# Starting a second feed-forward layer five slots earlier and its last product two slots later, in a fused attention and two-layer kernel

## The chip, the cores and the metric

The kernel runs on one core of one Trainium2 chip. The metric is the device time of one execution in microseconds (us). The engines are PE (matrix products; PEld is its weight load), DVE (vector work), ACT (activations and copies), POOL and SP; in this kernel SP issues most of the DMAs and POOL issues the others.

## The reference

Attention with a local window and 32 global keys per head feeds a feed-forward layer with the activation `h * sigmoid(h)`, and that feeds a second one with `h * cos(h)`. Both layers have 2304 rows, a width of 512 and an inner width of 2048.

```python
def _moe_ref(x, w_in, w_out):
    h = x @ w_in
    g = h * (1.0 / (1.0 + np.exp(-h)))
    return (g @ w_out).astype(np.float32)

def _moe2_ref(x, w_in, w_out):
    h = x @ w_in
    g = h * np.cos(h)
    return (g @ w_out).astype(np.float32)

x = attention(...)          # (4 * 544, 512)
x = _moe_ref(x, moe_w_in, moe_w_out)
return _moe2_ref(x, moe2_w_in, moe2_w_out)
...
```

## The kernel before, in words

Each fp32 operand is split into a high and a low part, and each product is made of three matmuls: low by high, high by high, high by low. Tokens lie on the moving side. The program is written out as a plan of **slots**: `at(rank, slot, function, ...)` puts a piece of work in a slot, and the pieces are issued slot by slot, by rank within one. From slot 36 on every engine runs its instructions exactly in that order. An instruction that waits therefore holds up all that stand behind it on its engine, and that is true of SP's and POOL's DMA issues too.

**First layer.** Tokens are taken in six tiles of 512, 256, 256, 256, 384 and 512. For each of 16 blocks `f` of the inner width, `gemm1(t, f)` makes h (12 matmuls), `silu` and `split_g` make g (ACT tanh, DVE, ACT cast, DVE), and `gemm2(t, f)` adds g times the second weights into the output banks (12 matmuls), one slot pair later. A wide tile has two slots for each f, a 256 tile one. Attention units for later tiles are slipped in between. Slots 80 to 111 hold the 384 tile, slots 112 to 143 the last one. Slot 144 is called `base`.

**Weight conversion.** The second layer's weights arrive as 64-bit words. In the slots between, 64 pieces are loaded (`load_w2_words`, an SP DMA into `raw`, a ring of two buffers), prepared by ACT (`rebias`, L131 and L132), put together by DVE (`to_f32`, L138 and L142) and stored by SP (`store_w2`).

**Second layer.** Three token tiles of 768, 768 and 640 columns; the inner width is taken in 8 pairs of blocks, so there are 24 pairs `q`. The first product of a pair is a 2 by 2 block scheme with seven products of half the size (`product(q, j)`, 6 matmuls of 384 or 320 columns, one per slot), whose left operands are precomputed into DRAM (`w1c`) and brought in by POOL (`stream`). `take` moves each result from PSUM into h. From h a chain of DVE and ACT instructions makes the two rows of g: `turns`, `rest`, `cosine`, `times_h`, `split_g2` (L701 to L730). `gemm2_second(q, row, c)` multiplies g, 128 tokens by 512 (3 matmuls), spread over seven slots among the products of the next pairs. With pair q's products in slots s to s+6, the chain starts in slot s+6 and `gemm2_second` in slot s+10. Loads of output weights (`load_w2`) and of the next tile's tokens (`load_right`) are on SP. `finish(5)` stores the last output of the first layer.

Of the kernel before, what the change touches and what calls it, by code (L numbers as in the profile page):

```python
# [11 lines left out]
F32 = mybir.dt.float32  # L12
F32R = mybir.dt.float32r
I32 = mybir.dt.int32
# [9 lines left out]
NF = DFF // 128  # L24
# [24 lines left out]
def attention_then_two_ffn(  # L49
# [9 lines left out]
    nc = tc.nc  # L59
# [3 lines left out]
    work = ctx.enter_context(tc.tile_pool(name="work", bufs=1))  # L63
# [5 lines left out]
    ps_a = ctx.enter_context(tc.tile_pool(name="ps_a", bufs=4, space=PSUM))  # L69
# [42 lines left out]
    HALF = NF // 2  # L112
# [3 lines left out]
    def slot(part, f, dtype=F32):  # L116
        return wts.tile([128, 1024], dtype, tag=f"w{part}_{f}", name="w")
# [57 lines left out]
    def bank_h(name, which=None):  # L175
        if which is None:
            which = turn[0] = 1 - turn[0]
        return ps_h.tile([128, 512], F32, tag=f"h{which}", name=name)
# [368 lines left out]
    L = {}  # L547

    def open_second():
        pool = ctx.enter_context(tc.tile_pool(name="second", bufs=1))  # L550
        area = pool.tile([128, 6400], F32, name="area")
        more = pool.tile([128, 1024], F32R, name="more")
        L["t"] = [area[:, i * 768 : i * 768 + 768] for i in range(3)]
        L["c8"] = [area[:, 2304 + i * 1024 : 3328 + i * 1024] for i in range(2)]
        L["out"] = [area[:, 4352 + i * 1024 : 5376 + i * 1024].bitcast(F32R) for i in range(2)]
        L["h"] = [area[:, 2304 + i * 768 : 3072 + i * 768] for i in range(4)]
        L["k"] = [area[:, 5376:6144].bitcast(I32)]
        L["raw"] = [xp.tile([128, NP * 384], F32, tag=f"x{x}1", name="raw") for x in "hl"]
        L["x"] = {}
        L["a"] = [more[:, i * 512 : i * 512 + 512] for i in range(2)]  # L560

    def open_products():
        for f in (14, 15):
            a = slot(0, f, F32R)
            L["a"] += [a[:, 0:512], a[:, 512:1024]]

    def open_rest():
        L["k"].append(work.tile([128, 768], I32, tag="act2", name="k"))
        L["r"] = [work.tile([128, 768], F32, tag=f"act{i}", name="r") for i in range(2)]
        L["g"] = [  # L570
            (x[:, 0:768], x[:, 768:1536])
            for x in (xp.tile([128, 1536], F32R, tag=f"x{x}0", name="g") for x in "hl")
        ]

    def load_left(i):
        if i == MOVE:
# [32 lines left out]
                out=w1c[i][LEFT.index(name)], in_=o[:, c].rearrange("p s x -> p (s x)").bitcast(F32)  # L609
            )  # L610

    def stream(q):
        nc.gpsimd.dma_start(out=L["a"][q % 6], in_=w1c[q // 7 % HALF][q % 7])  # L613

    def halves_of(t):
        n = size[1][t] // 2
# [42 lines left out]
    def product(q, j):  # L659
        n = size[1][q // HALF] // 2  # L660
        whole = j in (0, 1, 3, 4, 5)
        if whole:
            CH[q, j] = bank_h("ps_p", (q + j) % 2)[:, 0:n]
        bank = CH[q, {2: 0, 6: 4}.get(j, j)]
        a = L["a"][(7 * q + j) % 6].rearrange("p (s k x) -> p s k x", s=2, k=2)
        for k in range(2):
            hi, lo = a[:, 0, k], a[:, 1, k]
            xh, xl = right_parts(q // HALF, j, k)
            nc.tensor.matmul(bank, lo, xh, start=whole and k == 0, stop=False, skip_group_check=True)  # L669
            nc.tensor.matmul(bank, hi, xh, start=False, stop=False, skip_group_check=True)  # L670
            nc.tensor.matmul(bank, hi, xl, start=False, stop=k == 1, skip_group_check=True)  # L671
# [47 lines left out]

    def g_parts(q, row):  # L720
        n = size[1][q // HALF]
        return [x[:, 0:n] for x in L["g"][1 - row]]

    def split_g2(q, row, part):
        hi, lo = g_parts(q, row)
# [30 lines left out]
    EARLY = 2 * NP  # L756
    PAUSE = 6
    LEAD, SLACK, LOADS, AHEAD, FIRST, CUT = 9, 3, 6, 8, -4, 36
    POOLED = (0, 1, 2, 3, 4, 6, 8, 10)
    head, pre, gemm, pe, post = -20, 0, 10, 20, 40  # L760
    seq = [(t, f) for t in range(len(size[0])) for f in range(NF)]
# [3 lines left out]
    base = tick[-1]  # L765
# [7 lines left out]
    def at(rank, i, fn, *args):  # L773
        plan.setdefault(i, []).append((rank, fn, args))
# [83 lines left out]

    ends = [second[seq.index((t, NF - 1))] for t in range(len(SPANS))]
    free = [s for s in range(ends[0] + 3, last + 2) if all(not e <= s <= e + 2 for e in ends)]  # L860
    order = [(f, part) for i in range(HALF) for f in (i, i + HALF) for part in range(2)]
    order += [(f, part) for i in range(HALF) for f in (i + HALF, i) for part in (2, 3)]
    for i, (f, part) in enumerate(order):
        s = free[i * len(free) // len(order)]
        at(pre + 1, s - 1, load_w2_words, f, part)
        at(post - 1, s, rebias, 1, f, part)
        at(pre, s + 1, to_f32, 1, f, part)
        at(post - 1, s + 1, store_w2, f, part)
# [9 lines left out]
    for i, (t, f) in enumerate(seq):  # L878
# [11 lines left out]
        if f == NF - 1:  # L890
            at(post, second[i] if late < 0 else base + 3, finish, t)

    tiles, pairs = len(size[1]), HALF * len(size[1])
    at(pre, base + 2, load_sine)
    at(gemm - 1, base - 6, open_products)
    at(pre - 3, base + 5, open_rest)
    for i in range(HALF):
        s, wait, step = (last + 2 + 9 * i // 2, 2, 2) if i < 6 else (base + 12 + 8 * (i - 6), 3, 3)
        at(post, s, load_left, i)
# [2 lines left out]
            at(pre + 3, s + wait + g // 2 * step, split_left, i, g)  # L902
            at(pre - 1, s + wait + 1 + g // 2 * step, store_left, i, g)
    for t in range(tiles):
        s = base + 7 * HALF * (t - 1)
        for side in range(2):
            at(post, last + 2 if t == 0 else s + 8, load_right, t, side)
        for i in range(4):
            at(pre + 4, last + 4 + i if t == 0 else s + 22 + 7 * i, right_sum, t, i)
        for j in range(7):  # L910
            s_j = last + 4 * j + 5 if t == 0 else s + 7 * HALF - 6 + j
            for k in range(2):
                at(pre - 2 if t else pre + 5, s_j, split_right, t, j, k)
    for q in range(pairs):
        s = base + 7 * q
        final = q == pairs - 1
        for j in range(7):
            at(post, s + j - 6, stream, 7 * q + j)
            at(gemm, s + j, product, q, j)
            at(post, s + j, take, q, j)  # L920
        for row, b in ((1, s + 6), (0, s + 7)):
            at(pre, b, turns, q, row)
            at(pre, b, rest, q, row, 0)
            at(pre - 1, b + 1, rest, q, row, 1)
            at(pre + (0.2 if row else 0.1), b + 1, cosine, q, row, 0)
            at(pre - 0.5, b + 2, cosine, q, row, 1)
            at(pre, b + 3, times_h, q, row)
            at(pre, b + 3, split_g2, q, row, 0)
            at(pre - 1.5, b + 4, split_g2, q, row, 1)
        blocks = size[1][q // HALF] // 128  # L930
        todo = [(row, c) for row in (1, 0) for c in range(blocks)]
        for m, (row, c) in enumerate(todo):
            s_m = s + 10 + m * 7 // len(todo)
            if q == pairs - 2:
                s_m = s + 14 + m // 5
            at(gemm + 20, s_m, gemm2_second, q, row, c)
            if q % HALF == HALF - 1 and row == 0:
                at(post + 1, s_m, finish_second, q // HALF, c)
# [109 lines left out]
```

## Time and profile before

| | |
|---|---|
| median of 3 runs | 919.82 us (918.25 to 922.47) |
| profiled execution, device time | 922.28 us |
| its span, first to last instruction | 920.5 us |
| PE busy | 875.6 us (95%) |
| DVE, ACT, POOL busy | 664.1, 520.7, 166.0 us |
| mean granted TensorE clock | 0.991 |

PE is busy for nearly the whole span, so what can be won without fewer matmuls is the time in which it stands still or runs at the lower clock. The profiled execution took 2.5 us more than the median. A busy matmul is counted with its tail: a 512-column one is shown as 0.39 us, but in an unbroken run the next starts 0.22 to 0.23 us after it.

### The profile page before, as it was taken

The numbers are of one execution on the slowest core, as the hardware profiler recorded it, in microseconds if no ns is written. First come the engines' busy times: TensorE is split into PE (matmuls) and PEld (weight loads), VectorE is DVE, ScalarE is ACT, GpSimd is POOL, SyncE is SP. The second block draws the span as 40 slices with busy tenths as digits, with TensorE's granted clock in tenths as the row PEclk, the third lists the DMA queues.
The fourth block names the chain that finished last, engine by engine and source line by source line (L and its number), as shares of the span: only waits on it lengthen the run. The fifth ranks groups of instructions, "written<-read, shape, count | busy, mean of one in ns | idle before, by whom it ended". The sixth has DMA issues, their size and how long they took to land.

```text
span 920.5 us, 16535 instructions
## 1 busy us (share of the span) xinstructions
PE 875.6 (95%) x5838; PEld 761.0 (83%) x5838; DVE 664.1 (72%) x1547; ACT 520.7 (57%) x1171; POOL 166.0 (18%) x283
## 2 busy tenths in 40 slices
PE   8899899999999999998999989999899999899997
PEld 5667678989898999987878868889789988788886
DVE  4799996688887775676477648887776767766665
ACT  4989843567575564555345445564654545544553
POOL 2220110021222120011000021222122222222220
PEclk9999999999999999999999999999999999999999
DMA  8968410566565564544665677965366444365551
GB/s 259 332 208 295 158 44 12 179 187 196 158 211 165 159 200 133 153 140 150 217 211 194 213 232 235 268 196 138 92 169 186 116 122 118 96 192 142 143 126 57
DMA packets 101985, 156.53 MB, mean 170 GB/s; under 512 B 26384, under 2 KB 40208, under 8 KB 101904
## 3 DMA queue, kind: packets, MB, share of 16 engines
q1 hardware_dynamic: 77712, 111.44, 37.1%
q0 software_dynamic: 24192, 44.05, 18.7%
q8 instruction: 46, 0.75, 0.3%
q14 instruction: 35, 0.29, 0.1%
HBM read 123.47 MB, written 31.98 MB: 169 GB/s over the span
## 4 chain that ended last, share of the span: by engine, by line
PE 64%; DVE 12%; ACT 8%; DMA 8%; issue 2%; SPq 1%; POOL 0%; ACTq 0%; DVEq 0%
PE ps_y L740 6%; PE ps_y L741 5%; PE ps_y L742 5%; PE ps_y L520 5%; DMA raw<-in_w_dram 5%; PE ps_y L521 5%; PE ps_y L522 5%; PE ps_p L669 5%; PE ps_p L670 5%; PE ps_p L671 4%; PE ps_hid L483 4%; PE ps_hid L481 4%; PE ps_hid L482 4%; DVE r L705 2%; PE ps_o L354 1%
## 5 line engine op out<-in xcount | busy, mean ns | idle before, releaser
L520 PE MATMUL ps_y<-act,w 128*128 128x256 f32 (+2 forms) x384 | 133.3, 347 | 2.4 <-ACT act L499 2.4
L522 PE MATMUL ps_y<-act,w 128*128 128x256 f32 (+2 forms) x384 | 128.1, 334 | 0.5 <-DVE act L501 0.3
L521 PE MATMUL ps_y<-act,w 128*128 128x256 f32 (+2 forms) x384 | 127.7, 332 | 0.0
L481 PE MATMUL ps_hid<-xh,w 128*128 128x256 f32 (+2 forms) x384 | 126.2, 329 | 0.0
L483 PE MATMUL ps_hid<-xl,w 128*128 128x256 f32 (+2 forms) x384 | 126.1, 328 | 0.0
L482 PE MATMUL ps_hid<-xh,w 128*128 128x256 f32 (+2 forms) x384 | 126.0, 328 | 0.0
L740 PE MATMUL ps_y<-w,g 128*128 128x512 f32 x272 | 108.8, 400 | 13.0 <-DVE g L730 12.9
L741 PE MATMUL ps_y<-w,g 128*128 128x512 f32 x272 | 108.1, 397 | 0.0
L742 PE MATMUL ps_y<-w,g 128*128 128x512 f32 x272 | 108.0, 397 | 0.0
L613 POOL DMA_DIRECT2D w<-w1c x112 | 59.4, 530 | 246.2 <-PE ps_p L671 175.2
L520 PEld LDWEIGHTS ps_y<-act,w 128*128 128x128 f32 x384 | 73.4, 191 | 14.1 <-issue 4.5
L522 PEld LDWEIGHTS ps_y<-act,w 128*128 128x128 f32 x384 | 73.7, 192 | 7.9 <-DVE act L501 2.7
L493 DVE SCALAR_TENSOR_TENSOR act<-act,ps_hid 128x256 f32<-128x256 f32 (+2 forms) x96 | 50.6, 527 | 38.6 <-ACT act L492 38.0
L481 PEld LDWEIGHTS ps_hid<-xh,w 128*128 128x128 f32 x384 | 73.5, 191 | 5.7 <-issue 0.4
L483 PEld LDWEIGHTS ps_hid<-xl,w 128*128 128x128 f32 x384 | 73.2, 191 | 5.4 <-DVE xl L367 0.3
L521 PEld LDWEIGHTS ps_y<-act,w 128*128 128x128 f32 x384 | 73.7, 192 | 4.8
L482 PEld LDWEIGHTS ps_hid<-xh,w 128*128 128x128 f32 x384 | 73.3, 191 | 5.0
L499 ACT CAST act<-act 128x256 fp32r<-128x256 f32 (+2 forms) x96 | 47.4, 494 | 51.8 <-DVE act L493 39.0
L669 PE MATMUL ps_p<-w 128*128 128x384 f32 (+1 forms) x224 | 73.7, 329 | 2.5 <-DVE area L690 0.9
L492 ACT ACTIVATE act<-ps_hid 128x256 f32<-128x256 f32 (+2 forms) x96 | 44.7, 466 | 54.4 <-PE ps_hid L483 54.1
L670 PE MATMUL ps_p<-w 128*128 128x384 f32 (+1 forms) x224 | 73.5, 328 | 0.0
L671 PE MATMUL ps_p<-w 128*128 128x384 f32 (+1 forms) x224 | 73.2, 327 | 0.0
(139 smaller groups left out, 1957.2 us busy)
## 6 DMA issues: line engine op xcount, KB each, us to landing
w<-w1c POOLq DMA_DIRECT2D x112, 256.0 KB, 2.9
w<-in_w_dram SPq DMA_DIRECT2D x32, 512.0 KB, 7.3
raw<-in_w_dram SPq DMA_DIRECT2D x64, 256.0 KB, 3.2
more<-w1c POOLq DMA_DIRECT2D x56, 256.0 KB, 2.9
w2f<-w SPq DMA_DIRECT2D x64, 128.0 KB, 3.1
qk<-in_units_dram SPq DMA_DIRECT2D x24, 320.0 KB, 3.9
w1c<-area SPq DMA_DIRECT2D x28, 256.0 KB, 2.4
w1c<-w SPq DMA_DIRECT2D x28, 256.0 KB, 2.6
```

The lines of the kernel that those rows point to most:

```text
L481: nc.tensor.matmul(h, lo[:, ws], xh[:, k, :], start=k == 0, stop=False)
L482: nc.tensor.matmul(h, hi[:, ws], xh[:, k, :], start=False, stop=False)
L483: nc.tensor.matmul(h, hi[:, ws], xl[:, k, :], start=False, stop=k == NP - 1)
L520: nc.tensor.matmul(o, lo[:, ds_], gh, start=f == 0 and d % per == 0, stop=False, skip_group_check=True)
L521: nc.tensor.matmul(o, hi[:, ds_], gh, start=False, stop=False, skip_group_check=True)
L522: nc.tensor.matmul(o, hi[:, ds_], gl, start=False, stop=f == NF - 1, skip_group_check=True)
L669: nc.tensor.matmul(bank, lo, xh, start=whole and k == 0, stop=False, skip_group_check=True)
L670: nc.tensor.matmul(bank, hi, xh, start=False, stop=False, skip_group_check=True)
L671: nc.tensor.matmul(bank, hi, xl, start=False, stop=k == 1, skip_group_check=True)
L740: nc.tensor.matmul(y, gl, hi, start=begin_, stop=False)
L741: nc.tensor.matmul(y, gh, hi, start=False, stop=False)
L742: nc.tensor.matmul(y, gh, lo, start=False, stop=end)
```

## The change

1. All of the second layer but the loads and the precomputation of its left operands and weights starts five slots earlier: `onset = base - 5` takes the place of `base`. The first five products of pair 0 stand among the last four `gemm1` and `gemm2` of the first layer. Pair 0 uses two banks of another pool (`L["bank"]`) than the first layer's h.
2. `LAG = 12`: `gemm2_second` of a pair begins in slot s+12, not s+10. A third buffer for g is opened. The intermediate tiles `k` and `r` move to other places.
3. The streamed left operand has no ring of six buffers any more. It goes into the unused last 256 columns of the two tiles that hold the right operand of product j, as two DMAs of half the size.
4. The 64 weight conversions are spaced otherwise: one in each free slot up to the start of the 384 tile, then two in three slots. The plan has 28 of them in slots 80 to 111 before and 20 now; six come from slot 112 on, where none stood before. The load of a piece may be issued two slots ahead and not one.

Except for the streams, which are twice as many, each engine has the same instructions as before, in another order.

```diff
-        area = pool.tile([128, 6400], F32, name="area")
-        more = pool.tile([128, 1024], F32R, name="more")
+        area = pool.tile([128, 6912], F32, name="area")
...
-        L["k"] = [area[:, 5376:6144].bitcast(I32)]
+        L["k"] = [area[:, 5376 + i * 768 : 6144 + i * 768].bitcast(I32) for i in range(2)]
...
+        L["bank"] = [ps_a.tile([128, 512], F32, tag="a", name="ps_p") for _ in range(2)]
...
+    def open_third():
+        L["g"].append([work.tile([128, 768], F32R, tag=f"act{i}", name="g") for i in (1, 2)])
...
-    def stream(q):
-        nc.gpsimd.dma_start(out=L["a"][q % 6], in_=w1c[q // 7 % HALF][q % 7])
+    def left_parts(j):
+        return [L["x"][j, k][:, 768:1024] for k in range(2)]
+
+    def stream(q, j):
+        for i, part in enumerate(left_parts(j)):
+            nc.gpsimd.dma_start(out=part, in_=w1c[q % HALF][j][:, i * 256 : i * 256 + 256])
...
-            CH[q, j] = bank_h("ps_p", (q + j) % 2)[:, 0:n]
+            CH[q, j] = (bank_h("ps_p", (q + j) % 2) if q else L["bank"][j % 2])[:, 0:n]
...
-        return [x[:, 0:n] for x in L["g"][1 - row]]
+        return [x[:, 0:n] for x in L["g"][(2 * q + 1 - row) % 3]]
...
+    LAG = 12
...
+    slow = [s for s in range(ends[3] + 3, base) if (s - ends[3]) % 3 != 2 and not ends[4] <= s <= ends[4] + 2]
+    times = [s for s in free if s < ends[3]] + slow
...
-        s = free[i * len(free) // len(order)]
-        at(pre + 1, s - 1, load_w2_words, f, part)
+        s = times[i]
+        ready = max([times[i - 2] + 1 if i > 1 else 0, s - 2] + [e + 1 for e in ends if e < s])
+        at(pre + 1, ready, load_w2_words, f, part)
...
+    onset = base - 5
...
-        s = base + 7 * q
+        s = onset + 7 * q
...
-            at(post, s + j - 6, stream, 7 * q + j)
+            at(post, s + j - 6 if q else max(s + j - 6, last + 4 * j + 6), stream, q, j)
...
-            s_m = s + 10 + m * 7 // len(todo)
+            s_m = s + LAG + m * 7 // len(todo)
```

**PE, the first `gemm2_second` of pair 0.** Before, these rows stand there; `w_6351` and `w_6354` hold the right operand of product 3 of pair 1, `w_6549` the streamed left one.

```order
L669 MATMUL ps_p_6801<-w_6351,w_6549 128x384
L670 MATMUL ps_p_6801<-w_6351,w_6549 128x384
L671 MATMUL ps_p_6801<-w_6351,w_6549 128x384
L669 MATMUL ps_p_6801<-w_6354,w_6549 128x384
L670 MATMUL ps_p_6801<-w_6354,w_6549 128x384
L671 MATMUL ps_p_6801<-w_6354,w_6549 128x384
L740 MATMUL ps_y_6808<-w_6452,g_6732 128x512
```

Now it follows on product 5 of pair 1, whose right operand is in `w_6529` and `w_6532`, with the left one in the same two tiles.

```order
L671 MATMUL ps_p_6828<-w_6529,w_6532 128x384
L672 MATMUL ps_p_6828<-w_6529 128x384
L673 MATMUL ps_p_6828<-w_6529 128x384
L671 MATMUL ps_p_6828<-w_6532 128x384
L672 MATMUL ps_p_6828<-w_6532,w_6529 128x384
L673 MATMUL ps_p_6828<-w_6532,w_6529 128x384
L742 MATMUL ps_y_6835<-w_6453,g_6715 128x512
```

The consumer of g has moved two products further from the product that its chain starts from.

**SP, the end of the first layer.** `x_5` is the last output of the first layer, `raw<-x` the tokens of the second tile (`load_right`), `w2f_1_111` and `w2f_1_95` the output weights of blocks 9 and 1 (`load_w2`). Lines with - are of before, with + of the change.

```order
 L534 DMA x_5_91<-y 128x512 x4
+L634 DMA raw<-x_2_88 128x4x256
+L634 DMA raw<-x_3_89 128x4x128 x2
+L634 DMA raw<-x_4_90 128x4x256
 L152 DMA w<-w2f_1_111 128x512
-L632 DMA raw<-x_2_88 128x4x256
-L632 DMA raw<-x_3_89 128x4x128 x2
-L632 DMA raw<-x_4_90 128x4x256
 L152 DMA w<-w2f_1_95 128x512
```

The weights of block 9 were issued ahead of the four token loads, and now stand behind them.

**POOL, the streams in the middle of the second layer**, with the names that each issue waits for. Before:

```order
L613 DMA w<-w1c_6_130 128x512 [waits DMASW0_49,PE_49]
L613 DMA w<-w1c_0_131 128x512 [waits DMASW1_49,PE_49]
L613 DMA w<-w1c_1_132 128x512 [waits DMASW2_49,PE_49]
L613 DMA w<-w1c_2_133 128x512 [waits DMASW3_49,PE_49]
L613 DMA more<-w1c_3_134 128x512 [waits DMASW4_49,PE_49]
```

Now:

```order
L615 DMA w<-w1c_4_128 128x256 [waits DMASW0_49,PE_49]
L615 DMA w<-w1c_4_128 128x256 [waits DMASW1_49]
L615 DMA w<-w1c_5_129 128x256 [waits DMASW2_49,PE_49]
L615 DMA w<-w1c_5_129 128x256 [waits DMASW3_49]
L615 DMA w<-w1c_6_130 128x256 [waits DMASW4_49,PE_49]
L615 DMA w<-w1c_6_130 128x256 [waits DMASW5_49]
```

The names DMASW0 to DMASW7 go round, so that an issue waits for the DMA eight issues back: eight streams back before, four streams back now.

## Rows read from the trace of the kernel before

**Rows 1.** Stages: busy us of each engine, granted clock, DMA share, GB/s.

```profile
354.70:441.90 87.20, 80.10 (x569) 74.74 (x568) 56.47 (x164) 45.40 (x130) 8.54 (x8) 1.00 0.48 148
441.90:531.40 89.50, 86.37 (x373) 70.41 (x371) 57.59 (x107) 40.84 (x78) 3.40 (x6) 0.98 0.61 210
531.40:920.50 389.10, 369.46 (x1848) 325.89 (x1848) 270.26 (x389) 204.12 (x304) 85.86 (x162) 0.99 0.56 154
```

**Rows 2.** PE's waits in 531.4 to 920.5: us, times, longest.

```profile
PE ps_y L740 <- DVE g L730: 12.9, 10, 3.5
PE ps_p L669 <- DVE act L493: 1.5, 1, 1.5
PE ps_p L669 <- DVE area L690: 0.9, 1, 0.9
PE ps_p L669 <- ACT area L678: 0.8, 1, 0.8
```

**Rows 3.** PE's waits in 354.7 to 441.9, the 384 tile.

```profile
PE ps_o L347 <- POOL pgt L210: 6.2, 4, 2.3
```

**Rows 4.** ACT by line in the 384 tile: busy us, mean ns, idle before.

```profile
L131 ACT ACTIVATE raw<-raw 128x256 f32<-128x256 f32 x26 | 11.4, 439 | 29.9 <-DMA raw<-in_w_dram 27.5 <-DVE st L268 1.3 <-DVE w L142 1.1
```

**Rows 5.** Timeline of SP and ACT, one round of a conversion buffer.

```profile
436.15 0.33 SPq L126 DMA_DIRECT2D raw<-in_w_dram  x1
...
439.21 0.43 ACT L131 ACTIVATE raw<-raw 128x256 f32<-128x256 f32 x1 [1.57 <-DMA raw<-in_w_dram]
...
441.53 0.33 SPq L126 DMA_DIRECT2D raw<-in_w_dram  x1
```

**Rows 6.** Windows of 2 us, columns as in group 1.

```profile
652.00:654.00 2.00, 0.00 (x0) 0.00 (x0) 0.73 (x2) 2.00 (x5) 0.53 (x1) 1.00 0.58 160
654.00:656.00 2.00, 0.78 (x2) 0.69 (x3) 2.00 (x4) 0.16 (x1) 0.00 (x0) 0.71 0.22 69
656.00:658.00 2.00, 2.00 (x7) 1.52 (x6) 1.10 (x2) 1.28 (x3) 0.00 (x0) 0.50 0.00 0
658.00:660.00 2.00, 2.00 (x11) 1.86 (x10) 2.00 (x4) 1.41 (x3) 0.40 (x1) 0.94 0.00 0
...
788.00:790.00 2.00, 2.00 (x8) 2.00 (x7) 1.43 (x3) 1.52 (x5) 0.00 (x0) 0.50 0.00 0
```

**Rows 7.** Timeline of PE: start us, us, instruction, idle before it.

```profile
648.74 0.33 PE L669 MATMUL ps_p<-w 128*128 128x384 f32 x1
648.91 0.34 PE L670 MATMUL ps_p<-w 128*128 128x384 f32 x1
...
649.79 0.39 PE L740 MATMUL ps_y<-w,g 128*128 128x512 f32 x1
650.01 0.40 PE L741 MATMUL ps_y<-w,g 128*128 128x512 f32 x1
...
909.30 0.50 PE L740 MATMUL ps_y<-w,g 128*128 128x512 f32 x1 [0.32 <-DVE g L730]
```

**Rows 8.** Timeline of ACT and DVE: first and last piece of pair 0's chain.

```profile
544.64 0.85 ACT L701 ACTIVATE area<-area 128x768 int32<-128x768 f32 x1 [3.24 <-DVE area L688]
...
552.47 0.96 DVE L730 TENSOR_TENSOR g<-r,g 128x768 fp32r<-128x768 f32 x1 [1.27 <-ACT g L728]
```

**Rows 9.** Timeline of DVE at the start of the last tile.

```profile
460.24 0.96 DVE L640 TENSOR_TENSOR area<-raw 128x768 f32<-128x768 f32 x1 [4.17 <-DMA raw<-x]
```

**Rows 10.** PE's waits in 441.9 to 531.4, the last tile.

```profile
PE ps_y L520 <- ACT act L499: 1.6, 1, 1.6
```

**Rows 11.** DMA issues of 545 to 560: count, KB each, median us to landing.

```profile
w<-w2f SPq DMA_DIRECT2D x4, 256.0 KB, 10.0
w<-w1c POOLq DMA_DIRECT2D x4, 256.0 KB, 6.0
```

**Rows 12.** DMA queue of POOL, and its issues, in 531.4 to 920.5.

```profile
q0 software_dynamic: 23616, 43.00, 43.1%
...
w<-w1c POOLq DMA_DIRECT2D x108, 256.0 KB, 2.9
```

More of the change, by code (lines that the diff above doesn't have):

```diff
@@ L556, in open_second @@
         L["h"] = [area[:, 2304 + i * 768 : 3072 + i * 768] for i in range(4)]
-        L["k"] = [area[:, 5376:6144].bitcast(I32)]
+        L["k"] = [area[:, 5376 + i * 768 : 6144 + i * 768].bitcast(I32) for i in range(2)]
         L["raw"] = [xp.tile([128, NP * 384], F32, tag=f"x{x}1", name="raw") for x in "hl"]
         L["x"] = {}
-        L["a"] = [more[:, i * 512 : i * 512 + 512] for i in range(2)]
     def open_products():
-        for f in (14, 15):
-            a = slot(0, f, F32R)
-            L["a"] += [a[:, 0:512], a[:, 512:1024]]
+        L["bank"] = [ps_a.tile([128, 512], F32, tag="a", name="ps_p") for _ in range(2)]
     def open_rest():
-        L["k"].append(work.tile([128, 768], I32, tag="act2", name="k"))
-        L["r"] = [work.tile([128, 768], F32, tag=f"act{i}", name="r") for i in range(2)]
+        L["r"] = [slot(0, NF - 2)[:, 0:768], work.tile([128, 768], F32, tag="act0", name="r")]
         L["g"] = [
@@ L662, in product @@
         if whole:
-            CH[q, j] = bank_h("ps_p", (q + j) % 2)[:, 0:n]
+            CH[q, j] = (bank_h("ps_p", (q + j) % 2) if q else L["bank"][j % 2])[:, 0:n]
         bank = CH[q, {2: 0, 6: 4}.get(j, j)]
-        a = L["a"][(7 * q + j) % 6].rearrange("p (s k x) -> p s k x", s=2, k=2)
+        a = [x.rearrange("p (k x) -> p k x", k=2) for x in left_parts(j)]
         for k in range(2):
-            hi, lo = a[:, 0, k], a[:, 1, k]
+            hi, lo = (x[:, k] for x in a)
             xh, xl = right_parts(q // HALF, j, k)
@@ L891, in attention_then_two_ffn @@
             at(post, second[i] if late < 0 else base + 3, finish, t)
+    onset = base - 5
     tiles, pairs = len(size[1]), HALF * len(size[1])
     at(pre, base + 2, load_sine)
-    at(gemm - 1, base - 6, open_products)
-    at(pre - 3, base + 5, open_rest)
+    at(gemm - 1, onset, open_products)
+    at(pre - 3, base + 1, open_rest)
+    at(pre - 3, base + 5, open_third)
     for i in range(HALF):
@@ L904, in attention_then_two_ffn @@
     for t in range(tiles):
-        s = base + 7 * HALF * (t - 1)
+        s = onset + 7 * HALF * (t - 1)
         for side in range(2):
```

## The prediction

> **What bounds the kernel now.** I read the windows by stage first. PE is busy for 80.1 of 87.2 us in the 384 tile, 86.4 of 89.5 in the last tile of the first layer and 369.5 of 389.1 in the second layer [rows 1]. The reader is to see that PE is the bound everywhere, that no matmul is taken away, and that 7.1, 3.1 and 19.6 us of standing still are all there is to win in these stages, with the low clock besides.
>
> The view of waits, engine PE, then tells what PE stands for. In the second layer it is g: ten waits, 12.9 us, the longest 3.5, and three shorter ones ahead of products at the seam of the two layers [rows 2]. In the 384 tile it is four waits for POOL's part of the attention keys [rows 3]. POOL there waits for ACT; so I looked at ACT by line: it stands 27.5 us for the landing of raw weight words [rows 4]. The last view is that of 2 us windows, for the clock: after PE had done nothing in 652 to 654, the granted clock is 0.71, 0.50 and 0.94 in the three windows from 654 on, which is 1.2 GHz for part of each; at 788 it is 0.50 again [rows 6].
>
> **How long a slot is.** Matmuls of 384 columns start 0.17 us apart, those of 512 columns 0.22 [rows 7] (0.23 over longer runs). A product is 6 x 0.17 = 1.04 us, a block of `gemm2_second` 3 x 0.23 = 0.69. A pair of a 768 tile has 7 products and 12 blocks: 7.3 + 8.3 = 15.6 us, 2.23 for a slot.
>
> A stall costs more than its shown gap: a 512-column matmul is drawn 0.39 long but followed after 0.22 [rows 7], so some 0.17 us of pipelining is lost with each wait. I add that per wait removed.
>
> **The change, part by part.**
>
> *Distance 12.* The chain from the first `turns` to the last `split_g2` of a row lasts from 544.64 to 552.47 + 0.96, which is 8.8 us [rows 8]. Before, between the product that it starts from (j = 5) and the first `gemm2_second` PE has products 6, 0, 1, 2, 3 and 6 blocks of the pair before: 5.2 + 4.1 = 9.3 us. That is just above 8.8, so any other work on DVE or ACT makes PE wait. The longest wait of 3.5 us means a chain of about 12.8. Now seven products and 12 blocks lie between: 15.6 us. Even the longest chain fits, with 2.8 us to spare. Only the last pair keeps its wait of 0.3 [rows 7], since behind its products nothing is left to fill with. So 12.9 - 0.3 = 12.6 us go, and 9 x 0.17 = 1.5: **-14.1**. The bounds: all of it, or -8 if the longest waits (where the next tile's operands are split by the same engines) stay in part. The third g buffer makes this distance possible and costs no instruction. What is late next is nothing on PE: h has four buffers, and is read before it is written again.
>
> *Clock.* Each of the two low stretches, at 654 and 788, loses (0.29 + 0.50 + 0.06) x 2 = 1.7 us of full clock [rows 6], of which some falls in the wait itself; I take 1.5 each, **-3.0**. The waits before them should be gone. From below it is nothing, if the clock falls after some other wait, from above -3.4.
>
> *Seam.* The first product waited 1.5 us for the first layer's last bank of h, two others 0.9 and 0.8 for the `take` two products back [rows 2]. Pair 0 now has its own banks, and its first five products stand between `gemm1` and `gemm2` pieces, where a `take` has over 2 us. But products 2 to 4 of pair 1 now stand in slots with nothing beside them, and `take(1, 1)` is behind `finish(5)`'s copy on DVE. I leave 1.5 us of waits: 3.2 - 1.5, and two lost restarts of 0.17: **-2.0**, between -3.7 and 0. Pair 0's chain has 7 products and four half `gemm2` of 1.4 us before its consumer, 12.8 us against 8.8 and the load of the sine table.
>
> *384 tile.* A buffer of the conversion ring makes a round in 441.53 - 436.15 = 5.4 us: 3.1 from the issue to ACT's start, ACT, DVE, next issue [rows 5]. With two buffers that is 2.7 us for each conversion, and 28 of them make 75 of the stage's 87.2 us, while ACT has little else. Since ACT takes its work in order, the attention keys stand behind such a wait. With 20 conversions the ring needs 54 us, and each load is out two slots ahead (over 4 us against 3.1). The 6.2 us of waits [rows 3] should nearly go: 6.2 - 0.5, and 4 x 0.17: **-6.4**, between -6.9 and -2 (part of the lateness is of the attention itself).
>
> *Last tile of the first layer.* Six conversions come into it, each two instructions of 0.44 us or a little less on ACT [rows 4] and as many on DVE, whose share there is 57.6 of 89.5 us [rows 1]. But five of them fall where DVE has just stood 4.17 us for the first token load and PE 1.6 in turn [rows 9, 10]. That wait stays. Five more conversions are 4.3 us of DVE in seven slots of some 2.7 us, in which by its mean share it has 12 of 19 us to do; part falls into its waits for ACT's cast. A g of this tile has a slot pair (5.4 us) of room, so I take **+0.5**, between 0 and +4.
>
> *Weights behind tokens.* SP issues the output weights of block 9 behind four token loads. Loads of such weights in that crowd took 10.0 us [rows 11]. ACT and DVE split them three slots later, 6.7 us; ACT then stands 3.3 us in its queue, and behind it the cosines of pair 1 and a `take`, behind DVE's half `take(2, 1)`. PE wants that bank two slots on, about 3.4 us after it could be read; 3.3 + 0.6 + 0.7 + 0.5 for wait, cast, difference and take leave 1.7. I take **+2.0**, between 0 and +5.
>
> *Streams.* 336 DMAs of 128 KB in place of 168 of 256 KB. POOL is busy for 85.9 of 389.1 us [rows 1] with 162 of these issues, and twice that fits. Its DMAs fill 43.1% of the DMA engines [rows 12]; by the bytes that stays, and even if every packet of half the size took as long as a whole one it would be 86%. The wait on a product is for the one seven back, not six, so a stream has a slot more. An issue now waits for the DMA four streams back. A stream lands after 2.9 us as a rule and after 6.0 in the crowd [rows 11, 12]; four in flight are one in 0.7 and one in 1.5 us, against a slot of 2.23. **0**, between 0 and +7.
>
> By the Trainium skill ("DMA: Bandwidth & Descriptors", section "Anatomy of one DMA — SWDGE (gpsimd) path") such a DMA has a fixed part of about 2.0 us and then its bytes at 436 GB/s: 2.6 us for 256 KB, which the trace's 2.9 agrees with, and 2.3 for a half. If the fixed parts came one behind the other, a stream would take 4.6 us, and the second layer 168 x 2.4 = 400 us more. The trace speaks against that: 162 landings of 2.9 us are 470 us, more than the 389 in which they lay, so they overlap.
>
> The sum: -14.1 - 3.0 - 2.0 - 6.4 + 0.5 + 2.0 = -23.0. From the profiled 922.3 that gives 899.3; the profiled run was 2.5 us above the median, so **897**.
>
> **The rivals.**
>
> *Given back.* The six conversions and the late weights cost their upper ends (+9 in place of +2.5): 903. For it speaks that DVE and ACT run in order and that a wait of 1.6 us already stands there [rows 10]; against it the free third of DVE in that stage. To this belongs that half of the gain in the 384 tile stays away: 900 to 906.
>
> *The g waits stay.* The chain could be late because ACT and DVE are late altogether, not because it starts late; then two more slots only move the wait. With 6 us of it left and one low clock: 905. Against it: DVE is busy 270 of 389 us and ACT 204 [rows 1], so they do not fall behind from pair to pair.
>
> *Streams bound the second layer; it ends slower.* The place is POOL's issue, which waits for the landing four streams back. The gain of 23 us spread over 168 slots is 0.14 us a slot, so it decides when a stream takes more than 2.37 us, a landing of 9.5 us throughout. At 10.0 us, which SP's loads show in the crowd [rows 11], a slot takes 2.5: 168 x 0.27 = 45 more, 942. If only some 28 slots of the crowd are so, +8: 905. Against it: 2.9 us as a rule [rows 12]. The Trainium skill ("DMA: Bandwidth & Descriptors", section "Bandwidth") asks for DMAs of 1 MiB and more, and would lead here too.
>
> *It does nothing.* If PE's waits only changed their names, 920. Against it: they are waits for work that stands a known distance ahead.
>
> **How the numbers follow.** The forecast, 890 to 901, has a chance of 0.68; given back, 900 to 906, 0.17; the g waits in part, or streams in the crowd, about 905, 0.09; streams as the bound 0.04; no change 0.02. The likeliest is 897. The lower end: all terms at their best make -28.1, 891.7 after the correction, and some 2 us are left for a run with fewer low clocks; the upper end takes in the second and part of the third case: 889 to 906 holds about 0.85. A change of 0.5%, 4.6 us, is about what a measurement of this kernel can tell from none. Faster 0.94, same 0.02, slower 0.04.
>
> **What would show it.** Waits of PE for g should be one of 0.3 us and none at the tile changes; the 2 us windows should show 1.00 in the second layer. ACT's wait for raw words in the 384 tile should fall from 27.5 us to a few, and the tile should take 80 to 81 us. After the token loads at the seam there should be an ACT wait of 3 to 4 us for weights. It would be wrong if products wait for streams, or if the start of the last tile shows new waits for g of several us.

## The result, and the profile after

The changed kernel took 910.64 us (median of 4 runs, 907.50 to 912.56) beside 921.03 us (4 runs, 918.25 to 922.47) for the kernel before: a ratio of 0.9887, 95% interval 0.9847 to 0.9928. It is faster by 10.4 us, a little over 1%. The forecast was 897, between 889 and 906: the sign was right, the size was not, and the time lies outside the range.

The profiled execution took 909.52 us with a span of 907.5, so 13.0 us of span are gone where the sum had 23.0. (It was 1.1 us below its median, the one before 2.5 above the median of the three runs I had; these 3.6 us and the missing 10.0 make the 13.6 between 897 and 910.6.)

First the stages of the changed kernel, in the columns of [rows 1]: the 384 tile, the last tile with the products that now stand in it, and the rest of the second layer.

```profile
358.10:436.20 78.10, 78.10 (x568) 75.08 (x567) 52.42 (x151) 41.57 (x118) 8.37 (x8) 1.00 0.44 135
436.20:516.80 80.60, 76.38 (x333) 61.23 (x332) 54.26 (x104) 39.26 (x79) 6.57 (x12) 1.00 0.72 237
516.80:907.50 390.70, 375.80 (x1891) 330.49 (x1889) 276.95 (x402) 206.48 (x312) 170.99 (x324) 1.00 0.62 157
```

The 384 tile has no idle PE left: 78.10 of 78.10 us. In the second layer the clock is 1.00 throughout, but PE still stands for 14.9 us, 4.1 of them after its last matmul (4.1 before, too). The waits of PE there, the answer to [rows 2] (L742 is what L740 was, L671 the first matmul of a product, L682 to L688 are lines of `take`):

```profile
PE ps_p L671 <- DVE area L686: 5.6, 5, 2.3
PE ps_p L671 <- DVE area L682: 1.7, 3, 0.8
PE ps_p L671 <- DVE area L688: 1.4, 2, 1.1
PE ps_p L671 <- ACT area L684: 1.2, 2, 0.8
PE ps_y L742 <- DVE g L732: 0.6, 1, 0.6
```

The ten waits for g are down to one of 0.6, where one of 0.3 was forecast. In their place stand twelve waits, 9.9 us, of a kind that [rows 2] has twice: a product waits until DVE or ACT has taken the result two products back out of the same PSUM bank. The last tile of the first layer has four waits for ACT's cast of g where [rows 10] had one:

```profile
PE ps_y L520 <- ACT act L499: 4.2, 4, 1.4
```

To see where the time went I cut the span at the start of the first matmul of a stage, the same matmul in each kernel, read from PE's timeline. Before the seam's second cut the changed kernel has issued three blocks of `gemm2_second` fewer; these 2.1 us come back at the end, so they are moved there in the table. The first of the ten waits for g lies ahead of pair 2, so 1.9 us of the -14.1 (the wait and its tail of 0.17) belong to the seam:

```profile
553.49 0.50 PE L740 MATMUL ps_y<-w,g 128*128 128x512 f32 x1 [1.77 <-DVE g L730]
```

| stage, us | before | after | forecast | measured |
|---|---|---|---|---|
| up to the 384 tile | 354.68 | 358.13 | 0 | +3.45 |
| 384 tile | 87.17 | 78.12 | -6.4 | -9.05 |
| last tile, its first 13 blocks | 74.35 | 76.69 | +0.5 | +2.34 |
| seam, from there to the first product of pair 2 | 45.40 | 39.25 (+2.1) | -1.9 (-2.0 + 2.0 - 1.9) | -4.05 |
| pairs 2 to 23 and the end | 358.90 | 355.30 (-2.1) | -15.2 | -5.7 |

Most of what is missing is in the last line. Windows of pairs 2, 3 and 4 show where, first of before, then of after with pair 5 behind them (columns as in [rows 1]):

```profile
561.60:578.40 16.80, 15.97 (x80) 14.06 (x78) 14.77 (x25) 10.44 (x16) 3.72 (x8) 1.00 0.71 207
578.40:595.10 16.70, 15.99 (x80) 13.92 (x78) 13.64 (x23) 9.88 (x16) 3.72 (x8) 1.00 0.86 254
595.10:612.50 17.40, 16.03 (x80) 14.09 (x80) 13.90 (x20) 9.36 (x13) 3.72 (x8) 1.00 0.80 243
```

```profile
552.20:568.30 16.10, 15.96 (x79) 14.04 (x78) 10.62 (x15) 9.29 (x14) 7.38 (x15) 1.00 0.87 244
568.30:587.40 19.10, 17.11 (x80) 13.70 (x79) 15.49 (x25) 9.50 (x14) 7.42 (x15) 1.00 0.82 241
587.40:606.70 19.30, 16.19 (x80) 13.91 (x79) 15.82 (x26) 10.44 (x17) 7.35 (x15) 1.00 0.82 231
606.70:622.40 15.70, 15.70 (x80) 14.11 (x79) 12.62 (x17) 9.02 (x13) 7.40 (x15) 1.00 0.77 194
```

An unbroken pair takes 15.7 us, as in the last row. Pairs 3 and 4 take 19.1 and 19.3, together 4.3 us more than before. DVE's work (third busy figure) was even over the three pairs, 14.8, 13.6 and 13.9; now it is 10.6, 15.5 and 15.8, as much as an unbroken pair is long. The timeline of DVE just before one of the waits, and PE's wait:

```profile
589.59 1.55 DVE L590 TENSOR_TENSOR w<-w 128x256 f32<-128x256 f32 x4
591.05 1.02 DVE L599 TENSOR_TENSOR w<-w 128x512 fp32r<-128x512 f32 x2
591.99 0.95 DVE L707 SCALAR_TENSOR_TENSOR r<-area,r 128x768 f32<-128x768 int32 x1
592.86 0.69 DVE L165 TENSOR_TENSOR w<-w 128x512 fp32r<-128x512 f32 x1
593.46 0.95 DVE L642 TENSOR_TENSOR area<-raw,area 128x768 f32<-128x768 f32 x1
594.33 0.55 DVE L682 TENSOR_TENSOR area<-area,ps_p 128x384 f32<-128x384 f32 x1
```

```profile
594.93 0.45 PE L671 MATMUL ps_p<-w 128*128 128x384 f32 x1 [0.78 <-DVE area L682]
```

Without a gap in 4.7 us DVE sums left operands (L590) and splits them (L599), does a part of the chain (L707), splits output weights (L165) and sums the next tile's tokens (L642); the take (L682) is last. The first, second and fourth of these are side work whose slots count from `base`. By `onset = base - 5` the pairs moved five slots against it, and the left operands of the last two pairs now fall into the pairs that also have the next tile's sums.

### The profile page after: what moved, and what is told of

Same layout as the page of the kernel before. It is cut to its first block, busy times and chain, and to the rows that moved or that the text cites. A ratio compares the mean times of both kernels' runs of the same rounds, so it can differ in the third digit from the quotient of the medians.

```text
span 907.5 us, 16685 instructions
## 1 busy us (share of the span) xinstructions
PE 872.6 (96%) x5838; PEld 757.5 (83%) x5838; DVE 665.4 (73%) x1547; ACT 517.9 (57%) x1171; POOL 254.1 (28%) x451
## 4 chain that ended last, share of the span: by engine, by line
PE 72%; DVE 11%; DMA 5%; ACT 4%; issue 2%; SPq 1%; POOL 0%; DVEq 0%; ACTq 0%
PE ps_y L520 6%; PE ps_y L522 6%; PE ps_y L521 5%; PE ps_y L743 5%; PE ps_y L744 5%; PE ps_y L742 5%; PE ps_hid L481 5%; PE ps_hid L483 5%; PE ps_hid L482 5%; PE ps_p L671 5%; PE ps_p L672 5%; PE ps_p L673 5%; PE ps_o L354 2%; DMA w<-w2f 2%; PE ps_s L252 1%
## 5 line engine op out<-in xcount | busy, mean ns | idle before, releaser
L615 POOL DMA_DIRECT2D w<-w1c x336 | 177.6, 534 | 272.3 <-PE ps_p L673 194.2
L671 PE MATMUL ps_p<-w 128*128 128x384 f32 (+1 forms) x336 | 111.4, 331 | 10.3 <-DVE area L686 5.6
L672 PE MATMUL ps_p<-w 128*128 128x384 f32 (+1 forms) x336 | 110.2, 328 | 0.0
L673 PE MATMUL ps_p<-w 128*128 128x384 f32 (+1 forms) x336 | 109.8, 327 | 0.0
L743 PE MATMUL ps_y<-w,g 128*128 128x512 f32 x272 | 107.5, 395 | 0.0
L744 PE MATMUL ps_y<-w,g 128*128 128x512 f32 x272 | 107.2, 394 | 0.0
L742 PE MATMUL ps_y<-w,g 128*128 128x512 f32 x272 | 106.3, 391 | 0.6 <-DVE g L732 0.6
L703 ACT ACTIVATE area<-area 128x768 int32<-128x768 f32 (+1 forms) x48 | 38.9, 811 | 103.9 <-DVE area L690 67.5
L493 DVE SCALAR_TENSOR_TENSOR act<-act,ps_hid 128x256 f32<-128x256 f32 (+2 forms) x96 | 50.6, 527 | 53.2 <-ACT act L492 52.7
L520 PEld LDWEIGHTS ps_y<-act,w 128*128 128x128 f32 x384 | 73.2, 191 | 16.5 <-ACT act L499 5.9
L209 POOL TENSOR_SCALAR pgt<-tg 32x512 fp32r<-32x512 f32 (+1 forms) x32 | 22.0, 688 | 225.0 <-DVE tg L203 155.0
L671 PEld LDWEIGHTS ps_p<-w 128*128 128x128 f32 x336 | 63.1, 188 | 24.2 <-DVE area L686 7.7
L522 PEld LDWEIGHTS ps_y<-act,w 128*128 128x128 f32 x384 | 73.2, 191 | 7.9 <-DVE act L501 2.8
```

What stands on the lines that cost most here:

```text
L520: nc.tensor.matmul(o, lo[:, ds_], gh, start=f == 0 and d % per == 0, stop=False, skip_group_check=True)
L522: nc.tensor.matmul(o, hi[:, ds_], gl, start=False, stop=f == NF - 1, skip_group_check=True)
L615: nc.gpsimd.dma_start(out=part, in_=w1c[q % HALF][j][:, i * 256 : i * 256 + 256])
L743: nc.tensor.matmul(y, gh, hi, start=False, stop=False)
L744: nc.tensor.matmul(y, gh, lo, start=False, stop=end)
```

## The experiments

All times are medians, beside the kernel before on the same chip; its medians in the three batches are 920.95, 922.27 and 921.52. The changed kernel's 910.64 is of a batch of its own (921.03 before), so differences to it go across batches. The durations of stages are of the one profiled execution of each.

**The distance of the second product** (distance 10). The changed kernel with one number put back.

```diff
-    LAG = 12
+    LAG = 10
```

> The changed kernel with LAG = 10, the distance of before; the rest of the change stays. If the longer distance only changed the name of a part of the waits (theory 'moved'): waits for g of about 8 to 10 us come back, those for takes fall from 10 to about 5, the second layer is 3 to 5 us longer, about 914. If the distance is worth what was forecast (14 us, with 3 for the clock): about 924. If it is worth nothing: 910.6.

923.34 us, ratio 1.0015 (0.9985 to 1.0046): the whole gain is gone. PE's waits for g are back:

```profile
PE ps_y L742 <- DVE g L732: 16.2, 11, 3.6
```

So the distance is worth 12.7 us in the medians. In the profiled executions it is 9.6, and 12.2 when counted from the seam on (406.8 beside 394.6; stretches of low clock at 579 and 651 are part of it). It does what was forecast of it, but is worth less than the 14.1 + 3.0. Beside the waits for g, those for takes are 2.2 us here and not 9.9: a part of the waits only changed its name.

**The spacing of the conversions alone** (spacing). The kernel before with part 4 of the change and nothing else.

> The kernel before with nothing but the new spacing of the 64 weight pieces. The 384 tile should take 78 us and not 87. Theory 'the last tile gives part back': the last tile is 2 to 4 us longer than the 74.4 of before with waits of PE for ACT's cast, the whole about 914 to 916. Rival 'the seam takes it all': what is gained in the 384 tile comes back as waits at the seam and in the second layer, about 919 to 921.

916.66 us, ratio 0.9945 (0.9917 to 0.9973), about 4.3 us. The 384 tile takes 78.12 us, exactly as in the changed kernel: this term belongs to the spacing alone. The last tile already has three waits for the cast of g, 3.1 us.

**Half streams.** The kernel before, each stream as two DMAs of 128 KB into its old ring.

```diff
-        nc.gpsimd.dma_start(out=L["a"][q % 6], in_=w1c[q // 7 % HALF][q % 7])
+        for i in range(0, 512, 256):
+            nc.gpsimd.dma_start(out=L["a"][q % 6][:, i : i + 256], in_=w1c[q // 7 % HALF][q % 7][:, i : i + 256])
```

> The kernel before with one thing changed: each stream of a left operand is issued as two DMAs of 128 KB instead of one of 256 KB, into the same ring of six buffers. Theory 'streams are free': 920 to 922, no product waits for a DMA, and pairs 2 to 4 take what they took before (50.9 us). Rival 'streams cost' (more issues on POOL and more packets slow the other loads): pairs 2 to 4 grow by 1 us or more and the time by 3 or more.

922.04 us, ratio 0.9996 (0.9966 to 1.0026); pairs 2 to 4 take 16.79, 16.69 and 15.75 us, and no product waits for a DMA. The issues land after 2.4 us:

```profile
w<-w1c POOLq DMA_DIRECT2D x216, 128.0 KB, 2.4
```

Twice the number costs nothing here. By the Trainium skill ("DMA: Bandwidth & Descriptors", section "Measured (HBM→SBUF, 128 partitions, SWDGE, issued from GpSimd)") DMAs should be batched to 1 MiB or more; that is a rule for bandwidth, and these streams are needed one in a slot of 2.23 us. The landing of 2.4 us is near 2.3, an estimate from the fixed part and the bytes that the same page of the Trainium skill gives (section "Anatomy of one DMA — SWDGE (gpsimd) path").

**Takes before the side work** (takes first). The changed kernel with the side work of the second layer ranked behind the takes of its slot, in the same slots.

```diff
-            at(pre, s, split_w_hi, 1, f, 1)
+            at(post + 1 if i else pre, s, split_w_hi, 1, f, 1)
...
-        at(pre + 2, s + wait, left_sums, i)
+        at(pre + 2 if i < 6 else post + 2, s + wait, left_sums, i)
...
-                at(pre - 2 if t else pre + 5, s_j, split_right, t, j, k)
+                at(post + 5 if t else pre + 5, s_j, split_right, t, j, k)
```

> The changed kernel, with the second layer's side work (left_sums and split_left of pairs 6 and 7, right_sum and split_right of the later tiles, split_w of the output weights) issued behind the take of its slot and not ahead of it. Theory 'in order': PE's waits for takes (10 us in the changed kernel) arise because side work stands ahead of the take on DVE and ACT; pairs 3 and 4 then fall from 19.1 and 19.3 us to about 16.5, pairs 7 and 15 to about 16, the waits for takes in the second layer from some 9 us to under 3, and the time from 910.6 to about 904. Theory 'DVE is full': DVE has 15.5 us of work in these pairs, a pair without waits takes 15.7, so order can't help; pairs 3 and 4 stay above 18.5 and the time within 2 us of 910.6.

908.73 us, ratio 0.9852 (0.9804 to 0.9899), which can't be told from the changed kernel. Pair 4 falls from 19.32 to 17.81 us, but pair 3 is still 20.27 (a stretch of low clock lies in it) and pairs 8 to 14, the first of the next tile among them, take 2.4 more. The order within a slot is at most a part of it; the amount of work in these pairs stays as it was.

**Spread.** The changed kernel with the side work in other slots: the left operands of the last two pairs 14 slots apart, and the sums of the next tile's tokens later.

```diff
-        s, wait, step = (last + 2 + 9 * i // 2, 2, 2) if i < 6 else (base + 12 + 8 * (i - 6), 3, 3)
+        s, wait, step = (last + 2 + 9 * i // 2, 2, 2) if i < 6 else (base + 10 + 14 * (i - 6), 3, 3)
...
-            at(pre + 4, last + 4 + i if t == 0 else s + 22 + 7 * i, right_sum, t, i)
+            at(pre + 4, last + 4 + i if t == 0 else s + (26, 39, 44, 47)[i], right_sum, t, i)
```

> The changed kernel, with the side work of the second layer put elsewhere: the left operands of the last two pairs come to slots that spread them over the pairs instead of lying in pairs 3 and 4, and the right operands of the second and third tile are prepared towards the end of the tile before, not in its middle. Theory 'piled up' (by starting five slots earlier the second layer moved against this side work, which fixed slots hold; DVE now has too much in pairs 3 and 4, and the taking of products stands behind it): pairs 2 to 4 fall from the 54.5 us of the changed kernel to 48.5 to 49.5, the waits for DVE's and ACT's taking there mostly go, and the time falls to 905 to 906. Rival 'DMA crowd' (the side work waits for its loads, wherever it stands): pairs 2 to 4 stay at 53 us or more and the time within 2 us of the changed kernel's 910.6.

906.00 us, ratio 0.9824 (0.9777 to 0.9870). Windows of pairs 2, 3 and 4:

```profile
552.60:570.20 17.60, 15.97 (x79) 14.04 (x78) 12.89 (x21) 9.34 (x14) 7.39 (x15) 1.00 0.92 263
570.20:585.90 15.70, 15.70 (x79) 14.11 (x79) 12.91 (x18) 9.60 (x14) 7.40 (x15) 1.00 0.93 271
585.90:602.70 16.80, 16.00 (x79) 14.04 (x78) 13.70 (x23) 9.30 (x14) 7.41 (x15) 1.00 0.61 154
```

DVE's work is even again (12.9, 12.9, 13.7), and the three pairs take 50.1 us and not 54.5. The DMA share is higher in the first two (0.92 and 0.93), so a busier DMA does not by itself hold the pairs up.

**Not earlier.** The changed kernel with `onset = base`: no overlap, all else as changed.

> The changed kernel with onset put back to base, so that the second layer starts where it did, with the distance of 12, the streams and the conversions of the change. Theory 'piled up': the side work is back in its old place beside the pairs, so that pairs 2 to 4 fall from 54.5 us to 48 to 50, while the seam loses what overlapping had won (2 to 4 us), and the whole comes to 908 to 912. Rival 'the longer distance makes the takes late by itself': pairs 2 to 4 stay at 53 us or more and the whole comes to 913 to 917.

906.71 us, ratio 0.9838 (0.9796 to 0.9880). Pairs 2, 3 and 4:

```profile
556.00:571.70 15.70, 15.70 (x79) 14.03 (x78) 13.77 (x23) 9.99 (x16) 7.38 (x15) 1.00 0.79 220
571.70:587.80 16.10, 16.03 (x80) 13.89 (x78) 14.07 (x23) 9.97 (x16) 7.46 (x15) 1.00 0.95 277
587.80:604.00 16.20, 16.20 (x79) 14.01 (x79) 13.99 (x20) 9.42 (x14) 7.33 (x15) 1.00 0.93 255
```

PE has no wait in them, at the same distance of 12. So the distance does not make these takes late; the five slots do. At the tile changes the waits for takes stay: pairs 7 and 15 take 18.60 and 17.26 us, as in the changed kernel. The seam takes 43.86 us here against 39.25: the overlap wins 4.6 us there and spends 6.5 in pairs 2 to 4. Some 1.7 of the 4.6 are a stretch of low clock in this seam, amid its waits:

```profile
549.00:551.00 2.00, 1.32 (x4) 1.32 (x5) 1.57 (x4) 0.83 (x1) 1.08 (x3) 0.56 1.17 373
```

The time is below what I expected (908 to 912), but its interval overlaps that of the changed kernel, so whether the overlap as it stands loses something or wins nothing is not settled.

**Late pieces.** The changed kernel with the last five conversions later in the last tile.

```diff
+    slow = [s for s in slow if s <= last] + list(range(last + 14, base, 2))
     times = [s for s in free if s < ends[3]] + slow
```

> The changed kernel, with the last five weight pieces in slots 126 to 134 and not 117 to 123. Theory 'pieces': the four waits of PE for ACT's cast in the last tile (4.2 us) come from these five pieces, two ways: on ACT and DVE, and on SP ahead of the stores of the left operands; one wait of 1.5 us stays, and the last tile goes from 76.7 to about 74 us, the whole to about 907 to 908. Rival 'crowd': the waits come from the token loads and the stores alone; no change, 910 to 911.

909.07 us, ratio 0.9847 (0.9794 to 0.9900), which can't be told from the changed kernel. The last tile takes 77.6 us (a stretch of low clock lies in it) and still has 4.7 us of waits for the cast, but not the same ones. The changed kernel has four at 20, 27, 34 and 41 us from the start of the tile; here the first stays, the other three (2.9 us) are gone, and a new one stands at 74, behind a wait of ACT for the load of another left operand:

```profile
501.98 1.05 ACT L598 CAST w<-w 128x512 fp32r<-128x512 f32 x2 [5.39 <-DMA w<-w2f]
506.41 0.50 PE L520 MATMUL ps_y<-act,w 128*128 128x512 f32 x1 [2.83 <-ACT act L499]
```

ACT's waits in these 13 blocks for the stores of left operands, first of the changed kernel, then here:

```profile
ACT area L598 <- DMA w1c<-area: 11.1, 7, 4.0
ACT area L598 <- DMA w1c<-area: 4.5, 4, 1.9
```

So the place of the five conversions does matter for the three waits in the middle, as the theory "pieces" had it, and the tile wins little or nothing because another wait comes up; what makes that load late is open.

**Sums later.** The changed kernel with the first use of the second layer's first tokens two slots later (they are those of its first tile; the expectations call them the second tile's).

```diff
-            at(pre + 4, last + 4 + i if t == 0 else s + 22 + 7 * i, right_sum, t, i)
+            at(pre + 4, last + 6 + i if t == 0 else s + 22 + 7 * i, right_sum, t, i)
...
-            s_j = last + 4 * j + 5 if t == 0 else s + 7 * HALF - 6 + j
+            s_j = last + 4 * j + 5 + 2 * (j == 0) if t == 0 else s + 7 * HALF - 6 + j
```

> The changed kernel with the first work on the second tile's tokens (right_sum and the first split_right at the start of the last tile of the first layer) two slots later. Theory 'token load' (DVE stands in front of a load that has not landed, and the first layer's activation waits behind it): DVE's 3.6 us for the tokens nearly goes, the first of PE's four waits for the activation goes too, and the last tile falls from 76.7 to 74.5 to 75.5 us; the time is 908 to 909.5. Rival 'stores' (the waits come from the stores of the sums, which ACT waits for later): the tile stays within 0.5 us of 76.7.

907.05 us, ratio 0.9826 (0.9771 to 0.9880), the last tile 74.58 us with a stretch of low clock in it. In the changed kernel, DVE stands for the tokens and the activation (L493) waits behind it, then PE:

```profile
453.95 0.96 DVE L642 TENSOR_TENSOR area<-raw 128x768 f32<-128x768 f32 x1 [3.60 <-DMA raw<-x]
454.83 0.68 DVE L493 SCALAR_TENSOR_TENSOR act<-act,ps_hid 128x512 f32<-128x512 f32 x1
...
456.21 0.49 PE L520 MATMUL ps_y<-act,w 128*128 128x512 f32 x1 [1.29 <-ACT act L499]
```

Two slots later the tokens are there, and the tile has one wait (one to three in the three kernels below):

```profile
458.44 0.95 DVE L642 TENSOR_TENSOR area<-raw 128x768 f32<-128x768 f32 x1
...
468.53 0.50 PE L520 MATMUL ps_y<-act,w 128*128 128x512 f32 x1 [1.80 <-ACT act L499]
```

One profile would not settle this, for the tile varies by up to 1.7 us between kernels in which it is alike. Over all of them: without the mend (changed kernel, takes first, distance 10, spread, not earlier) it takes 75.5 to 76.9 us, mean 76.4, and with it (this kernel and the three below) 73.8 to 75.6, mean 74.8. The ranges just touch, and the means put the standing for tokens at some 1.6 us of the tile. The spacing alone had brought three waits where before had one, and late pieces took three away; both causes act on ACT's cast, and the wait that is left is not put down to either.

**Both mends, and two variants.** *Spread and sums* joins spread and sums later. *Base and sums* is not earlier with sums later. *Rights behind* is spread and sums, with `split_right` of the later tiles ranked behind the takes (the last lines of the diff of takes first).

> The changed kernel with both mends that earlier runs bear out: the side work spread over the pairs, and the first work on the second tile's tokens two slots later. If the two losses are separate ones (side work on DVE in pairs 3 and 4; DVE standing before the token load in the last tile), the gains add: the last tile 74 to 75 us, pairs 2 to 4 at 49 to 50.5, and a median of 902.5 to 905. Rival: the time lost only moves from one to the other, and the median stays at 906 to 907.

> The changed kernel with onset put back to base (no overlap of the layers) and the first work on the second tile's tokens two slots later. By the theory that the overlap wins about 4 us at the seam once its side work is out of the way, this is behind the spread version by 0 to 3 us: 903.5 to 906. Rival (overlap wins nothing even when mended): it equals or beats the spread version.

> As the kernel with the side work spread and the sums later, and besides, the preparing of the next tile's right operands (split_right) ranked behind the taking of products. If the remaining waits at the two tile changes come from the order on DVE, pairs 7 and 15 fall from 18.6 and 17.3 us to 17 and 16.3 and the median by 1 to 2.5 us; if the operands are then late for the next tile's first products, the pairs after the change grow by as much and the median stays.

| on one chip | median, us | runs | ratio to before | interval |
|---|---|---|---|---|
| spread and sums | 901.35 | 897.25 to 904.16 | 0.9779 | 0.9745 to 0.9813 |
| base and sums | 903.35 | 902.30 to 912.13 | 0.9818 | 0.9776 to 0.9859 |
| rights behind | 901.05 | 900.27 to 902.36 | 0.9778 | 0.9749 to 0.9807 |

The two mends add: they gave 4.6 and 3.6 us below the changed kernel's median apart, and 9.3 together, and the interval of the ratio doesn't touch that of the change, which those of the two alone still overlap. This version beats both kernels. Beside base and sums, the overlap with its side work spread is worth 2.0 us, but the intervals overlap. Rights behind brings pairs 7 and 15 from 18.59 and 17.25 us to 17.48 and 16.33, and pairs 8 and 16, with which the next tile starts, from 15.96 and 14.65 to 16.85 and 15.53: what is won is given back within a pair, and the median stays, as the second half of its expectation said.

## Why the prediction was wrong, step by step

**The step that failed** is in *Distance 12*: "What is late next is nothing on PE: h has four buffers, and is read before it is written again." I looked at h, the output of the takes, and not at the PSUM bank that a take sets free, although *Seam* prices two such waits. A product needs the take of two products back, one slot of PE's time after it could be read, and takes stand in DVE's queue behind side work. The five slots, too, have a term at the seam alone, and none for the side work that stays in its slots while the pairs move. So waits for takes, 9.9 us, stand where those for g, 12.9 us, had stood, and -14.1 - 3.0 came out as -7.6 (-5.7 in the pairs and -1.9 at the seam). With the 3.0 of the clock counted as won, *Distance 12* is about -4.6, beyond its bound of -8.

Two places are shown. Pairs 2 to 4 take 54.5 us, where 47.1 (three unbroken pairs) was implied, and 48.0 without the five slots and 50.1 with the work spread: this loss is that of the five slots. Pairs 7 and 15, at the tile changes, take 2.9 and 1.6 us more than unbroken ones, in waits for takes, with the five slots and without; at distance 10 PE waits for g alone in these two pairs, so the distance uncovered those waits. My bound of -8, "if the longest waits stay in part", named the place and the engines, under another wait's name.

**Behind it stands a wrong use of an average.** Against the rival that the waits stay I wrote that DVE is busy 270 of 389 us. The average is right and still holds (277 of 391); in two pairs the share is 0.8 of a stretch that its own lateness has drawn out.

**Clock.** Right in this profile: no low stretch after 517. It is not so in every execution. *Sums later* has the same second layer, and in its profile the clock falls at 602 behind the 2.3 us wait for a take in pair 4, which takes 20.9 us there and not 19.3:

```profile
602.00:604.00 2.00, 2.00 (x7) 1.61 (x6) 1.36 (x3) 0.50 (x1) 1.05 (x2) 0.51 1.03 341
```

In the first part, for which I had no term, the profile of after has three such stretches and the one of before two, of some 1.7 us each [rows 6]. PE is busy there for 342.35 us and not 339.69, with the same matmuls, which is most of the +3.45; the idle time grew by 0.8 only. Profiles of kernels with the same first part have from one to five such stretches, so a single profile can't say whether the change has a share in it.

**384 tile.** The mechanism was right, and the term of -6.4 was mis-sized: -9.05, beyond its bound of -6.9. I had counted four waits, 6.2 us; the stage had a fifth, for ACT's cast of g, which went with them:

```profile
PE ps_y L520 <- ACT act L499: 0.8, 1, 0.8
```

The five show 7.0 us, so each cost 0.4 us that isn't drawn, where I had added 0.17; a part of that is told below, the rest is open. ACT's wait for raw words fell from 27.5 us [rows 4] to 2.1 in this line of ACT:

```profile
L131 ACT ACTIVATE raw<-raw 128x256 f32<-128x256 f32 x20 | 8.8, 438 | 2.2 <-DMA raw<-in_w_dram 2.1
```

**Last tile.** +0.5 was mis-sized; it measured +2.3, and the before it is compared with had a stretch of low clock at 464 in it, some 1.6 us, so +3.9 without it (half streams, with the first layer of before and no low stretch there, has 72.29, which makes +4.4). My upper bound was +4. I had seen DVE stand for the tokens [rows 9] and counted that standing as room for the conversions; it is the start of a delay that they prolong, for moving either of the two takes waits away. And I had counted the conversions as work of ACT and DVE alone: ACT's waits for the stores of left operands, 2.4 us before, are 7.7 with the spacing alone and 11.1 with the change.

**Seam.** -2.0 was right: without the wait for g, PE's waits there fell from 3.3 us to 1.6, where 1.5 was to be left. That the stage measured -4.05 and not -1.9 is the next term. **Weights behind tokens**, +2.0: the wait on ACT is there, 2.30 us and not 3 to 4,

```profile
557.26 0.62 ACT L161 CAST w<-w 128x512 fp32r<-128x512 f32 x1 [2.30 <-DMA w<-w2f]
```

but the view shows no wait of PE from there to 576, and pair 2 takes 16.1 us, 0.4 over an unbroken one: little or nothing of the +2.0 reached PE.

**Streams**, 0: right, shown by half streams, and no product of the changed kernel waits for one. By the time, the case that came nearest is *given back*, at its upper end of 906 and beyond it, though by takes more than by the two causes that I named. By the mechanism, *it does nothing* was nearer than its chance of 0.02 says: a large part of PE's waits changed their names.

## What to carry to other kernels

When a stage is moved in a plan written by slots, look at what stays behind: work whose slots count from a fixed point comes to lie on other pairs, and the load of each in-order engine has to be added up pair by pair, not over the stage. When a long wait is taken away, list every other resource that the same instruction needs (here the PSUM bank of two products back) and the margin of each, for the old wait had hidden them. Work that waits for a load should stand where the load has landed, above all on an engine that the critical work shares.

## What the runs showed of the hardware

A wait of PE costs more than its shown gap. The rows around one, after a block of `gemm2_second`, matmuls and then the weight loads:

```profile
575.48 0.39 PE L744 MATMUL ps_y<-w,g 128*128 128x512 f32 x1
576.56 0.45 PE L671 MATMUL ps_p<-w 128*128 128x384 f32 x1 [0.69 <-DVE area L682]
576.84 0.34 PE L672 MATMUL ps_p<-w 128*128 128x384 f32 x1
577.02 0.35 PE L673 MATMUL ps_p<-w 128*128 128x384 f32 x1
```

```profile
575.25 0.19 PEld L744 LDWEIGHTS ps_y<-w,g 128*128 128x128 f32 x1
576.56 0.19 PEld L671 LDWEIGHTS ps_p<-w 128*128 128x128 f32 x1 [1.12 <-DVE area L682]
576.67 0.19 PEld L672 LDWEIGHTS ps_p<-w 128*128 128x128 f32 x1
```

From 575.48 to 576.84 two matmuls take 1.36 us, where 0.23 + 0.17 is the unbroken pace: 0.96 us are lost where 0.69 is shown. Of the difference 0.17 is the drawn tail that I counted; the other 0.1 goes with the weight load. Within a run it lies under the matmul before; here it starts with its own matmul, at 576.56, and the next matmul follows after 0.28. By the Trainium skill ("TensorE: Matmul & The Clock Gate", section "Architectural detail: the array is 16× 32×32, not 1× 128×128") PE's queue can pull weight loads ahead of matmuls in flight; the trace agrees for unbroken runs, and shows that in this kernel a load whose matmul waits for a bank is not done ahead of that wait: in all eleven such waits of 0.3 us or more after 517, load and matmul start together. The profile puts the wait on the load too, so whether it could have gone ahead is not shown. I had not expected that; by an estimate with 0.27 and not 0.17 for the nine waits for g and the four of the 384 tile, the sum would have been 1.3 us larger in size, further from the result, so it is not what made it wrong.
